# Denominator sums of a linear-attention block: four quarters of PE's columns in place of two halves

## The chip, the cores and the metric

The kernel runs on one core of one Trainium2 chip. The metric is the device time of one execution in microseconds (us). The kernel before the change takes 1488.77 us, the median of 3 runs (1488.16 to 1489.85). Engine names are those of the profile: PE is TensorE's matmul (PEld its weight load), DVE is VectorE, ACT is ScalarE, POOL is GpSimd, SP is SyncE, which issues most of the DMAs.

## The reference, cut to what matters

Everything is float32, S = 2048 tokens and D = 576 features.

```python
xn = layernorm(x)
q, k, v = split_heads(xn @ wqkv)              # H = 32 heads of 18
phi = lambda t: where(t > 0, t + 1, exp(t)) + 1e-6
pq, pk = phi(q), phi(k)
kv  = einsum("hsd,hse->hde", pk, v)
z   = einsum("hsd->hd", pk)
num = einsum("hqd,hde->hqe", pq, kv)
den = einsum("hqd,hd->hq", pq, z) + 1e-6
s   = merge_heads(num / den) @ wo
g   = silu((gelu(xn @ w_gate) * (xn @ w_up)) @ w_down)      # 4608 wide
out = x + s * g
```

The change touches den, one number for each head and token (32 x 2048), and the division by it.

## The kernel before, in words

**Stages.** Up to about 190 us the kernel norms x, multiplies it with the k and v weights and sums kv and z over all tokens in one PSUM accumulation (kv_a, kv_b). In between and up to 231 us it computes q for four blocks of TBN = 512 tokens, and phi of it. At about 197 to 210 us kv is masked to its heads and multiplied with wo (kv_wo, L525), which gives the operand kvh, kvl and kv4 (high and low words, see below), and z is spread on the heads' columns: zc, a matrix with one column for each head. From 231 to 303 us the kernel divides phi(q) by den and multiplies it with that operand: that is s, stored in DRAM. From 303 to 1104 us follow the gate and up projections (with Winograd-like sums of blocks, names al, be, ga, de), and from then to the end the down projection (bd) and the output.

**Precision.** The large products use the one-pass type fp32r on words: ACT copies an operand with rounding (the high word), DVE subtracts it from the original (the low word), and PE adds up the products of the words. Products on plain f32 operands, den's among them, are told by the trace as two matmul instructions, each with a weight load of its own, for every matmul that the kernel writes.

**The division.** Features of q lie on the 128 rows (partitions) in NHG = 5 groups, tokens along the columns. For each block of tokens `den` (L612) is called once, `scale` (L634) for each of the five groups, `halve` (L642) to split the scaled phi(q) into words.

- `den` multiplies zc (128 rows x 64 columns) with phi(q) of the group, 5 groups added up in PSUM. The 64 columns of zc hold the 32 heads twice (the write of zc at the end of kv_wo has r = 2). The two halves of a block's tokens, HB = 256 each, go to the two halves of PE's columns: rows 0 to 63 of the PSUM bank d get the first half of the tokens, rows 64 to 127 the second, each half with its 32 sums twice, one copy below the other.
- DVE adds EPS to the bank into r (128 x 256) and takes the reciprocal.
- For each half, ACT copies the 64 rows into rd (in the tile aux) at the half's own columns, rounding to fp32r, and DVE overwrites the lower 32 rows of them with the low word, r minus the high word. So rd (128 x 512) holds on 32 rows the high words and on the 32 rows beside them the low words of one half, and zeros at the other half's columns, which `make_sel` (L574) writes once with POOL.
- `scale` multiplies rd with sel, a matrix of zeros and ones that adds up all rows of a head and spreads them on the head's features, into a bank b, and DVE multiplies phi(q) with it.

**Order.** Every engine gets its instructions in the order in which the kernel writes them (the helpers act, vec, mm, pool and dma, L121 to L134, pin each to the program's order). Around the change that order is written out by hand: den(2) stands after the first of the five products q of block 3, and scale(2) after the third, fourth and fifth (q_hold, L458); den(3), den(0) and den(1) stand each after the first of the four products s of the block before (s_mm, L662, 28 matmuls on two banks), with the scales after the second and third. Between them stand the builds of operands for the gate stage (xf to xo, 'T1', 'T2'). make_sel is called behind the last q of block 2. The PSUM banks d, b, q and s come from one rotation of six.

The four calls of den share one tile rd, and every helper's instructions have one line in the profile (L128 for PE, L125 for DVE, L122 for ACT, L131 for POOL, L134 for DMAs), so they are told apart by tiles.

Of the kernel before, what the change touches and what calls it, by code (L numbers as in the profile page):

```python
# [8 lines left out]
F32 = mybir.dt.float32  # L9
# [3 lines left out]
ALU = mybir.AluOpType  # L13
# [3 lines left out]
P = 128  # L17
# [3 lines left out]
H = 32  # L21
# [4 lines left out]
TBN = S // TB  # L26
# [4 lines left out]
NHG = 5  # L31
WIDTHS = [GW, GW, GW, GW, D - 4 * GW]
W4 = WIDTHS[4]


Q4 = 64
# [54 lines left out]
def block_kernel(ctx, tc, x, xe, wq_d, wkv_d, wo, wgu_d, wd_d, out):  # L91
# [6 lines left out]
    def bank(name):  # L98
        return ps.tile([P, 512], F32, tag="one", bufs=6, name=name)
# [4 lines left out]
    def big(i, shape, dt, name):  # L104
        return sb.tile(shape, dt, tag=f"b{i}", bufs=1, name=name)
# [7 lines left out]
    def gl_tile(shape, name, dt=F32):  # L113
        return sb.tile(shape, dt, tag="gl", bufs=6, name=name)

    def tmp(shape, name):
        return sb.tile(shape, F32, tag="tmp", bufs=4, name=name)
# [3 lines left out]
    def act(*args, **kw):  # L121
        pin(nc.scalar.activation(*args, **kw))  # L122

    def vec(op, *args, **kw):
        pin(getattr(nc.vector, op)(*args, **kw))  # L125

    def mm(*args, **kw):
        pin(nc.tensor.matmul(*args, **kw))  # L128

    def pool(op, *args, **kw):  # L130
        pin(getattr(nc.gpsimd, op)(*args, **kw))  # L131

    def dma(out, in_, eng=None):
        tc.keep_in_program_order((eng or nc.sync).dma_start(out=out, in_=in_))  # L134

    def split(hi, lo, src):
        act(hi, src, AF.Copy)
        vec("tensor_sub", lo, src, hi.bitcast(F32))
# [1 line left out]
    ident = sb.tile([P, P], F32, name="ident")  # L140
    make_identity(nc, ident)
    eps_t = sb.tile([P, 32], F32, name="eps_t")
    eps_t, zx = eps_t[:, 0:1], eps_t[:, 2:4]
    small = sb.tile([P, 640], F32, name="small")
    nc.gpsimd.memset(eps_t, LN_EPS)

# [321 lines left out]
    at = {}  # L468

    def band(m, src, pattern, c):  # L470
        nc.gpsimd.affine_select(
            out=m, in_=src, compare_op=ALU.is_ge, fill=0.0, base=0,
            pattern=[[-s, n] for s, n in pattern], channel_multiplier=c,
        )
        nc.gpsimd.affine_select(
            out=m, in_=m, compare_op=ALU.is_ge, fill=0.0, base=DH - 1,
            pattern=[[s, n] for s, n in pattern], channel_multiplier=-c,
        )

    def make_masks():  # L480
        ones = tmp([P, NHG * H], "ones")
        nc.gpsimd.memset(ones, 1.0)

        at["mask"] = mask = small[:, 0:GW]
        m3, o3 = (i.rearrange("p (h j) -> p h j", h=HG) for i in (mask, ones[:, 0:GW]))
        nc.gpsimd.affine_select(
            out=m3, in_=o3, compare_op=ALU.is_ge, fill=0.0, base=-1,
            pattern=[[-DH, HG], [0, DH]], channel_multiplier=1,
        )
        nc.gpsimd.affine_select(  # L490
            out=m3, in_=m3, compare_op=ALU.is_ge, fill=0.0, base=DH,
            pattern=[[DH, HG], [0, DH]], channel_multiplier=-1,
        )
        nc.gpsimd.memset(mask[0:1, :], 1.0)
        at["maskh"] = small[:, P : P + NHG * H].rearrange("p (g h) -> p g h", g=NHG)
        band(at["maskh"], ones.rearrange("p (g h) -> p g h", g=NHG), [[-GW, NHG], [DH, H]], 1)
        at["zc"] = small[:, P + NHG * H : P + 3 * NHG * H].rearrange("p (g h) -> p g h", g=NHG)
        nc.gpsimd.memset(at["zc"][Q4:P], 0.0)

    def kv_done():  # L500
# [24 lines left out]
    def kv_wo(gi):  # L525

        if gi == 4:
            at["kvh"] = big(4, [P, 4, D], F32R, "kvh")
            at["kvl"] = big(5, [P, 4, D], F32R, "kvl")

            at["kv4"] = big(6, [P, 4, D], F32R, "kv4")
            pool("memset", at["kv4"][Q4:P, 1, :].bitcast(F32), 0.0)
        kvh, kvl, kv4 = at["kvh"], at["kvl"], at["kv4"]
        zc, mh = at["zc"], at["maskh"]
        wdt, k = (W4, W4 + 1) if gi == 4 else (GW, GW + 1)
        w = at["wo4"] if gi == 4 else at["wo"][:, gi]
        pw = []
        for c, cs in enumerate((slice(0, HALF), slice(HALF, D + 2))):
            pw.append(bank(f"kw_{gi}_{c}"))
            mm(  # L540
                pw[c][0:wdt, 0 : cs.stop - cs.start], at["kvm"][0:k, gi, 0:wdt], w[0:k, cs],
                start=True, stop=True,
            )
        r, x_ = slice(0, Q4 if gi == 4 else GW), slice(Q4, W4)
        z = pw[1][:, HALF : HALF + 1]

        def parts(hi, lo, rows):
            for c in range(2):
                cs = slice(c * HALF, (c + 1) * HALF)
                split(hi[:, cs], lo[:, cs], pw[c][rows, 0:HALF])  # L550

        if gi == 4:
            vec("tensor_copy", zx[x_], z[x_].to_broadcast([W4 - Q4, 2]))
            parts(kv4[x_, 2, :], kv4[x_, 3, :], x_)
            for c in range(2):
                act(kv4[Q4:P, 0, c * HALF : (c + 1) * HALF], pw[c][r, 0:HALF], AF.Copy)

        vec(
            "tensor_scalar", zc[r, gi, :].rearrange("p (r h) -> p r h", r=2),
            mh[r, gi, None, :].to_broadcast([r.stop, 2, H]), z[r], None, op0=ALU.mult,  # L560
        )
        if gi == 4:
            parts(kv4[r, 0, :], kv4[r, 1, :], r)
        else:
            parts(kvh[r, gi, :], kvl[r, gi, :], r)

    def move_rows():
        for gi in range(4):
            r, e = slice(Q4 + 2 * gi, Q4 + 2 * gi + 2), slice(GW, P)
            dma(out=at["zc"][e, gi, :].rearrange("p (r h) -> p r h", r=2)[:, :, H - 1], in_=zx[r])  # L570
            for t, i in ((at["kvh"], 2), (at["kvl"], 3)):
                dma(out=t[e, gi, :].bitcast(F32), in_=at["kv4"][r, i, :].bitcast(F32))

    def make_sel():  # L574

        n = NHG * P
        buf = big(15, [P, n + TBN], F32R, "aux")
        at["sel"] = sel = buf[:, 0:n].rearrange("p (g j) -> p g j", g=NHG)
        at["rd"] = rd = buf[:, n : n + TBN]
        one = sb.tile([H, NHG, P], BF16, tag="tmp", bufs=4, name="self")  # L580
        pool("memset", one, 1.0)
        four, last = one[:, 0:4, 0:GW], one[:, 4, :].rearrange("p (r j) -> p r j", r=2)
        for o, pattern, base in ((four, [[GW, 4], [1, GW]], 0), (last, [[0, 2], [1, Q4]], 4 * GW)):
            pool(
                "affine_select",
                out=o, in_=o, compare_op=ALU.is_ge, fill=0.0, base=base,
                pattern=pattern, channel_multiplier=-DH,
            )
            pool(
                "affine_select",  # L590
                out=o, in_=o, compare_op=ALU.is_ge, fill=0.0, base=DH - 1 - base,
                pattern=[[-s_, n_] for s_, n_ in pattern], channel_multiplier=DH,
            )
        pool(
                "affine_select",
            out=one[:, 0:4, GW:P], in_=one[:, 0:4, GW:P], compare_op=ALU.is_ge, fill=0.0,
            base=1 - H, pattern=[[0, 4], [0, P - GW]], channel_multiplier=1,
        )
        for i in range(4):
            r = slice(i * H, (i + 1) * H)  # L600
            if i % 2:
                act(sel[r], one, AF.Copy)
            else:
                pool("tensor_copy", sel[r], one)
        for i in range(2):
            pool(
                "memset", rd[2 * H * i : 2 * H * (i + 1), HB * (1 - i) : HB * (2 - i)].bitcast(F32), 0.0
            )

    HB = TBN // 2  # L610

    def den(tb):  # L612

        pd = bank(f"d_{tb}")
        for gi in range(NHG):
            for i in range(2):
                mm(
                    pd[2 * H * i : 2 * H * (i + 1), 0:HB], at["zc"][:, gi, :],
                    ph[tb][:, gi, i * HB : (i + 1) * HB],
                    start=(gi == 0), stop=(gi == NHG - 1),  # L620
                )
        r = gl_tile([P, HB], f"r_{tb}")
        rd = at["rd"]
        vec("tensor_scalar", r, pd[:, 0:HB], EPS, None, op0=ALU.add)
        vec("reciprocal", r, r)
        for i in range(2):
            c = slice(i * HB, (i + 1) * HB)
            rows, low = slice(2 * H * i, 2 * H * (i + 1)), slice(H * (2 * i + 1), 2 * H * (i + 1))
            act(rd[rows, c], r[rows], AF.Copy)
            vec("tensor_sub", rd[low, c], r[low], rd[low, c].bitcast(F32))  # L630

    pqs, s_d, words = {}, {}, {}

# [629 lines left out]
    center(3)  # L1263
    v_post(1, 2)
    make_masks()

    def x_next(n):
# [22 lines left out]
    for n in range(3, 2 * TT):  # L1290
# [3 lines left out]
        if n >= TT:  # L1294
            j, c = divmod(n - TT, 2)
# [102 lines left out]
    for q in range(NQ):  # L1398
        g = q // 2
# [61 lines left out]
```

## Time and profile before

| what | value |
|---|---|
| median of 3 runs | 1488.77 us |
| profiled execution, its own time | 1488.81 us |
| its span, first to last instruction | 1487.1 us |
| mean granted TensorE clock | 0.998 |
| tile d on PE | 80 matmuls of 128x256, 215.1 to 275.4 us |
| DVE reciprocal | 4 of 1753 ns |

How to read it: the span is what the profile sees; the profiled execution's own time has 1.7 us more around it. Busy shares are those of the span. A row of a timeline has the start, the length from the first start to the last end, the engine, line and operation, out<-in tiles, the shape, and a count; in brackets stands the engine's idle time before it, and what ended it. A row of a tile view has the count, the shortest, median and longest duration in ns, and the first and last start. Matmuls are pipelined: each is longer than the distance to the next, so the distance of starts tells what one costs. A row of the chain of waits has a start, a length and who held the chain; SPq is SP's DMA queue.

### The profile page before, as it was taken

The page shows a single profiled execution, that of the slowest core. Times are in us where ns is not written, and L with a number is a line of the kernel's source. Part 1 is how long each engine was busy: PE and PEld are TensorE (multiplying, and loading weights), DVE is VectorE, ACT ScalarE, POOL GpSimd, SP SyncE. Part 2 cuts the span into 40 slices and gives each one's busy share as a digit, 9 for nine tenths or more (in the row PEclk, how much of TensorE's full clock was granted, in tenths as well). Part 3 has the DMA queues.
Part 4 walks back from the last instruction along what each step waited for, and adds up shares of the span by engine and source line. Part 5 has one row for each costly group of instructions (what it writes and reads, how often), then busy time and mean ns, then how long its engine had stood idle before and what let it go on. Part 6 is the DMA issues. An engine that isn't in the chain of part 4 may idle for free.

```text
span 1487.1 us, 21863 instructions
## 1 busy us (share of the span) xinstructions
PE 1471.1 (99%) x8128; PEld 1310.2 (88%) x8128; DVE 1145.7 (77%) x1587; ACT 560.1 (38%) x923; POOL 581.0 (39%) x515
## 2 busy tenths in 40 slices
PE   8999999999999999999999999999999999999998
PEld 8989988988888888888888888888889999999998
DVE  7567466557787788787878787788787988989887
ACT  5434335433223322323322223322234546455454
POOL 4342241124656757555675655757641000000000
PEclk9999999999999999999999999999999999999999
DMA  4425003452231522433242232422379888767886
GB/s 163 176 117 213 6 2 136 167 207 86 92 128 54 181 85 93 149 106 110 82 163 101 98 128 67 167 86 98 129 274 314 262 258 261 240 188 239 272 291 214
DMA packets 115132, 230.62 MB, mean 155 GB/s; under 512 B 10882, under 2 KB 42882, under 8 KB 112978
## 3 DMA queue, kind: packets, MB, share of 16 engines
q1 hardware_dynamic: 112370, 217.17, 43.5%
q0 software_dynamic: 2656, 12.06, 2.2%
q8 instruction: 64, 1.05, 0.3%
q14 instruction: 42, 0.34, 0.1%
HBM read 146.57 MB, written 82.58 MB: 154 GB/s over the span
## 4 chain that ended last, share of the span: by engine, by line
PE 95%; DVE 2%; DMA 1%; issue 1%; ACT 0%; SPq 0%; POOL 0%; DVEq 0%; POOLq 0%; ACTq 0%
PE bd L128 24%; PE ga L746 15%; PE de L746 15%; PE al L746 15%; PE kv L128 8%; PE be L746 7%; PE q L128 4%; PE s L128 4%; PE kv_a L128 1%; PE xt L205 1%; PE d L128 1%; DMA raw<-in_wgu_dram 0%; DVE wb L125 0%; DMA raw_b<-hs 0%; PE kw L128 0%
## 5 line engine op out<-in xcount | busy, mean ns | idle before, releaser
L131 POOL TENSOR_TENSOR sm<-raw 128x384 f32<-128x384 f32 x72 | 76.7, 1065 | 154.6 <-DMA raw<-in_wgu_dram 129.0
L128 PE MATMUL kv<-wkv,xo_B 128*128 128x384 f32 x672 | 127.6, 346 | 0.3 <-ACT xo_B L122 0.3
L125 DVE TENSOR_TENSOR wa<-sm,wa 128x768 fp32r<-128x768 f32 x72 | 93.0, 1291 | 36.1 <-ACT wa L122 35.3
L128 PEld LDWEIGHTS kv<-wkv,xo_B 128*128 128x128 f32 x672 | 119.4, 193 | 1.2 <-ACT xo_B L122 0.8
L128 PE MATMUL bd<-w_head,hi 128*128 128x288 f32 x516 | 118.0, 294 | 0.0
L125 DVE TENSOR_TENSOR wb<-raw,wb 128x256 fp32r<-128x256 f32 (+1 forms) x108 | 108.0, 1000 | 7.3 <-ACT wb L122 5.8
L125 DVE TENSOR_TENSOR wa<-raw,wa 128x256 fp32r<-128x256 f32 x72 | 64.8, 900 | 50.7 <-ACT wa L122 47.5
L122 ACT ACTIVATE hi<-raw_h 128x1024 fp32r<-128x1024 f32 x59 | 62.4, 1060 | 96.8 <-PE bd L128 64.0
L128 PE MATMUL bd<-w_end,hi 128*128 128x288 f32 x448 | 89.9, 294 | 0.0
L122 ACT ACTIVATE spot_h<-spot_h 128x512 f32<-128x512 f32 x49 | 30.8, 633 | 151.7 <-DVE spot_h L125 151.7
L125 DVE TENSOR_TENSOR raw_h<-raw_h,hi 128x1024 fp32r<-128x1024 f32 x59 | 71.7, 1219 | 20.6 <-ACT hi L122 20.5
L128 PEld LDWEIGHTS bd<-w_head,hi 128*128 128x128 f32 x516 | 87.0, 188 | 0.1
L128 PE MATMUL bd<-w_end,raw_h 128*128 128x288 f32 x264 | 77.9, 295 | 0.0
L122 ACT ACTIVATE u<-al 128x512 f32<-128x512 f32 x72 | 41.0, 592 | 90.1 <-PE al L746 81.8
L122 ACT ACTIVATE wa<-sm 128x1152 fp32r<-128x1152 f32 x36 | 41.8, 1161 | 81.6 <-PE de L746 71.0
L128 PEld LDWEIGHTS bd<-w_end,hi 128*128 128x128 f32 x448 | 71.9, 188 | 0.0
L128 PE MATMUL bd<-beside,raw_h 128*128 128x288 f32 x240 | 70.8, 295 | 0.0
L128 PE MATMUL q<-xo_B,wq 128*128 128x512 f32 x240 | 64.1, 395 | 0.0
L746 PE MATMUL ga<-xo_B,wb 128*128 128x512 f32 x252 | 63.3, 390 | 0.4 <-DVE u L125 0.4
L131 POOL TENSOR_TENSOR spot_h<-spot_h,spot_h 128x512 f32<-128x512 f32 x45 | 62.1, 1387 | 2.9 <-DVE spot_h L125 2.4
L746 PE MATMUL al<-xo_B,wa 128*128 128x512 f32 x252 | 63.0, 389 | 0.0
L746 PE MATMUL ga<-xr_B,wb 128*128 128x512 f32 x252 | 63.0, 389 | 0.0
(259 smaller groups left out, 4076.1 us busy)
## 6 DMA issues: line engine op xcount, KB each, us to landing
raw_h<-hs SPq DMA_DIRECT2D x176, 256.0 KB
raw<-in_wgu_dram SPq DMA_DIRECT2D x36, 768.0 KB
hs<-spot_h SPq DMA_DIRECT2D x90, 256.0 KB
hs<-spot_g SPq DMA_DIRECT2D x80, 256.0 KB
b<-in_wd_dram SPq DMA_DIRECT2D x42, 432.0 KB
hs<-spot_m SPq DMA_DIRECT2D x38, 256.0 KB
raw_g<-hs SPq DMA_DIRECT2D x22, 256.0 KB
kept_T<-xo_T SPq DMA_DIRECT2D x4, 1280.0 KB
```

The source lines that it names most:

```text
L122: pin(nc.scalar.activation(*args, **kw))
L125: pin(getattr(nc.vector, op)(*args, **kw))
L128: pin(nc.tensor.matmul(*args, **kw))
L131: pin(getattr(nc.gpsimd, op)(*args, **kw))
L205: pin(nc.tensor.transpose(xts[n][j][:, k, :], xs[:, j, k * P : (k + 1) * P], ident))
L746: nc.tensor.matmul(o, w[0:rows, wi, :], xop[0:rows, xi, :], start=(start and n == 0), stop=(n == len(PASSES) - 1), skip_group_check=True,)
```

## The change

den now cuts the 512 tokens of a block into four quarters of 128, one for each quarter (32 columns) of PE, and zc holds each head once. The bank d has 32 sums on each of four groups of 32 rows, r is 128 x 128. For each quarter ACT copies its 32 rows to rd at the quarter's own columns, and DVE writes the low words to the 32 rows beside it (the neighbour's rows, `i ^ 1`) at the same columns. rd is cleared whole. zc and the column of z that is moved by DMA have half the width.

The written matmuls of one den go from 10 (64 columns of weights, 256 tokens) to 20 (32 columns, 128 tokens), ACT's copies from 2 to 4, DVE's subtractions from 2 to 4. All else keeps its place in the order of its engine.

```diff
-    eps_t, zx = eps_t[:, 0:1], eps_t[:, 2:4]
+    eps_t, zx = eps_t[:, 0:1], eps_t[:, 2:3]
...
-        at["zc"] = small[:, P + NHG * H : P + 3 * NHG * H].rearrange("p (g h) -> p g h", g=NHG)
+        at["zc"] = small[:, P + NHG * H : P + 2 * NHG * H].rearrange("p (g h) -> p g h", g=NHG)
...
-            vec("tensor_copy", zx[x_], z[x_].to_broadcast([W4 - Q4, 2]))
+            vec("tensor_copy", zx[x_], z[x_])
...
         vec(
-            "tensor_scalar", zc[r, gi, :].rearrange("p (r h) -> p r h", r=2),
-            mh[r, gi, None, :].to_broadcast([r.stop, 2, H]), z[r], None, op0=ALU.mult,
+            "tensor_scalar", zc[r, gi, :], mh[r, gi, :], z[r], None, op0=ALU.mult,
         )
...
-            dma(out=at["zc"][e, gi, :].rearrange("p (r h) -> p r h", r=2)[:, :, H - 1], in_=zx[r])
+            dma(out=at["zc"][e, gi, H - 1 : H], in_=zx[r])
...
-        for i in range(2):
-            pool(
-                "memset", rd[2 * H * i : 2 * H * (i + 1), HB * (1 - i) : HB * (2 - i)].bitcast(F32), 0.0
-            )
-
-    HB = TBN // 2
+        pool("memset", rd.bitcast(F32), 0.0)
+
+    HB = TBN // 4
...
         for gi in range(NHG):
-            for i in range(2):
+            for i in range(4):
                 mm(
-                    pd[2 * H * i : 2 * H * (i + 1), 0:HB], at["zc"][:, gi, :],
+                    pd[H * i : H * (i + 1), 0:HB], at["zc"][:, gi, :],
                     ph[tb][:, gi, i * HB : (i + 1) * HB],
                     start=(gi == 0), stop=(gi == NHG - 1),
                 )
...
         vec("tensor_scalar", r, pd[:, 0:HB], EPS, None, op0=ALU.add)
         vec("reciprocal", r, r)
-        for i in range(2):
+        for i in range(4):
             c = slice(i * HB, (i + 1) * HB)
-            rows, low = slice(2 * H * i, 2 * H * (i + 1)), slice(H * (2 * i + 1), 2 * H * (i + 1))
+            rows, low = (slice(H * k, H * (k + 1)) for k in (i, i ^ 1))
             act(rd[rows, c], r[rows], AF.Copy)
-            vec("tensor_sub", rd[low, c], r[low], rd[low, c].bitcast(F32))
+            vec("tensor_sub", rd[low, c], r[rows], rd[rows, c].bitcast(F32))
```

## The prediction

> **What bounds the kernel now.** I read the page first (busy times and the chain that ended last), then the kernel in stretches, then the two tiles that the change touches, and last the timeline of each engine around one of the four calls of den.
>
> ```profile
> span 1487.1 us, 21863 instructions
> PE 1471.1 (99%) x8128; PEld 1310.2 (88%) x8128; DVE 1145.7 (77%) x1587; ACT 560.1 (38%) x923; POOL 581.0 (39%) x515
> ...
> PE 95%; DVE 2%; DMA 1%; issue 1%; ACT 0%; SPq 0%; POOL 0%; DVEq 0%; POOLq 0%; ACTq 0%
> PE bd L128 24%; PE ga L746 15%; PE de L746 15%; PE al L746 15%; PE kv L128 8%; PE be L746 7%; PE q L128 4%; PE s L128 4%; PE kv_a L128 1%; PE xt L205 1%; PE d L128 1%; DMA raw<-in_wgu_dram 0%; DVE wb L125 0%; DMA raw_b<-hs 0%; PE kw L128 0%
> ```
>
> PE is busy all the time, and the chain is 95% PE. Tile d, which den writes, is on that chain with 1%. The table by stretches shows where PE has any time to spare.
>
> ```profile
> 200.00:303.00 103.00, 102.94 (x669) 91.18 (x668) 60.09 (x96) 46.56 (x91) 21.89 (x28) 1.00 0.32 116
> 303.00:500.00 197.00, 197.00 (x872) 163.20 (x871) 143.29 (x199) 60.16 (x99) 105.32 (x86) 1.00 0.34 121
> ...
> 1090.00:1130.00 40.00, 35.69 (x222) 32.57 (x221) 35.85 (x39) 16.09 (x22) 16.89 (x23) 1.00 0.89 307
> ```
>
> After the length, the columns are PE, PEld, DVE, ACT and POOL busy, the granted clock, the DMA share and GB/s. All four dens lie in 200 to 303 us, where PE is busy for 102.94 of 103.00 us at clock 1.00. So a PE instruction taken out there shortens the run, as long as nothing else is late in its place.
>
> **What one den costs PE.** The tile view of d:
>
> ```profile
> L128 PEld LDWEIGHTS d<-ph,small x80: 132/137/138, 215.1 to 275.2; 128*64 128x64 f32 x80
> L128 PE MATMUL d<-ph,small x80: 378/379/431, 215.1 to 275.4; 128*64 128x256 f32 x80
> ...
>   DVE r L125: 7.4, 3
> ```
>
> Two stretches at the start of the first den, of tile d alone (PE, PEld, DVE):
>
> ```profile
> 215.06:215.08 0.02, 0.01 (x2) 0.01 (x2) 0.00 (x0) 1.00 0.00 0
> 215.08:215.30 0.22, 0.22 (x2) 0.18 (x4) 0.00 (x0) 1.00 0.00 0
> ```
>
> The timeline of PE, start and length first:
>
> ```profile
> 215.07 2.38 PE L128 MATMUL d<-ph,small 128*64 128x256 f32 x20
> 217.38 1.42 PE L128 MATMUL q<-xo_B,wq 128*128 128x512 f32 x5
> ...
> 201.50 2.11 PE L128 MATMUL kw<-wo_t,kvm 127*126 127x288 f32 x8
> ...
> 33.22 1.05 PE L128 MATMUL kv_a<-pk,va 128*127 128x126 f32 x8
> 34.10 0.29 PE L128 MATMUL kv_b<-pk,va 128*73 128x72 f32 x2
> ```
>
> The kernel writes 10 matmuls per den, 40 in all; the trace has 80, so each f32 matmul is two passes. From its first matmul to the next tile's, a den takes 217.38 - 215.07 = 2.31 us. What does a pass cost by its columns? Eight passes of kw take 2.11 us; with about 0.41 for the last, that is 1.70/7 = 0.243 us for 288 columns, 0.84 ns a column. Eight of kv_a with 126 columns: (1.05 - 0.27)/7 = 0.111, 0.88 ns a column. A pass of d with 256 columns should take 0.216 us, and 20 of them 4.3 us. They take half of it: the two halves of PE's columns work side by side. The stretches show it directly: two passes begin within 0.02 us, and no third one begins in the next 0.22.
>
> So a den is 10 slots of 0.216 us (2.16) and 0.15 us for the first weights and the change of shape at its end.
>
> **The change on PE.** A den now issues 20 matmuls, 40 passes of 128 columns, on four quarters. If the four work side by side as the two do, it is 10 slots of 0.11 us (kv_a's pass) and the same 0.15: 1.25 us, **1.06 us less**, wherever nothing else is late. Weights cost nothing of their own: the columns loaded per den stay 20 x 64 = 40 x 32, and they were hidden under the passes. The bounds: if no two quarters overlap, 40 x 0.11 + 0.15 = 4.55 us, 2.24 more than now; the good end is the 1.06 less. I take the good end: the nearest row, d itself, shows full overlap of its two parts, down to 0.216 against 0.216.
>
> **The change on DVE and ACT.** The tile view of r:
>
> ```profile
> L122 ACT ACTIVATE aux<-r x8: 414/417/418, 222.5 to 278.6; 64x256 fp32r<-64x256 f32 x8
> L125 DVE TENSOR_TENSOR aux<-r,aux x8: 415/418/423, 223.0 to 279.0; 32x256 fp32r<-32x256 f32 x8
> L125 DVE TENSOR_SCALAR r<-d x4: 411/425/425, 220.3 to 275.8; 128x256 f32<-128x256 f32 x4
> L125 DVE RECIPROCAL r<-r x4: 1753/1753/1754, 220.7 to 276.3; 128x256 f32<-128x256 f32 x4
> ```
>
> ACT, DVE and PEld around the first den, from their timelines:
>
> ```profile
> 217.53 1.49 ACT L122 ACTIVATE aux<-self 32x640 fp32r<-32x640 bf16 x2 [4.09 <-POOL self L131]
> ...
> 219.67 0.63 ACT L122 ACTIVATE e_q<-e_q 128x512 f32<-128x512 f32 x1
> ...
> 219.67 0.69 DVE L125 TENSOR_SCALAR ph<-q 128x512 f32<-128x512 f32 x1 [6.31 <-ACT e_q L122]
> 220.28 0.41 DVE L125 TENSOR_SCALAR r<-d 128x256 f32<-128x256 f32 x1
> ...
> 222.96 0.87 DVE L125 TENSOR_TENSOR aux<-r,aux 32x256 fp32r<-32x256 f32 x2 [0.48 <-ACT aux L122]
> ...
> 223.94 0.30 PEld L128 LDWEIGHTS b<-aux 128*128 128x128 f32 x2 [0.34 <-issue]
> ```
>
> With half the columns, DVE's add falls from 0.425 to about 0.29 (1.04 ns a column between this row and 0.69 at 512). The reciprocal is linear at best, 0.88, or 0.96 if 0.16 of it is fixed as in the add; I take 0.92. ACT's two copies become four: (0.63 - 0.417)/256 = 0.84 ns a column, so 0.31 each, 1.34 with the gaps against 0.86. The last subtraction falls from 0.42 to 0.29. DVE's four subtractions run behind the copies, one each. Sum of the chain from add to last low word: 0.14 + 0.83 + 0.13 - 0.48 = **0.62 us shorter**.
>
> That matters in the first den alone. In the other three DVE begins its add when PE is done (the 7.4 us, 3 times); the matrix product that follows den covers the chain already, and the chain gets shorter. In the first den DVE is held by its in-order queue: before the add stands ph, which starts at 219.67 after ACT's e_q, which stands behind two copies of self that ACT got from POOL at 217.53. Nothing of this moves when PE finishes d earlier. So the add still starts at 220.28, the low words are ready at 223.83 - 0.62 = 223.21, and b's weights load 0.11 later, at 223.32 against 223.94. PE would be there at 222.9, and waits about 0.45 us: **this den is worth 0.62, not 1.06**.
>
> **What is hidden or too small.** The five products for zc shrink, DVE has time there; the four row moves are as many, with half the elements; POOL clears rd in one memset in place of two, the same element count, long before ACT's first copy, which now waits for it. The order of the instructions on each engine is otherwise unchanged.
>
> **A stall that goes.** In the second and third den, building the next operand stands behind ACT's copies, and so does the product of ph and b, and then ACT's emptying of an s bank.
>
> ```profile
> 241.23 1.49 ACT L122 ACTIVATE xo_T<-xf_B 128x1536 fp32r<-128x1536 f32 x1
> ...
> 246.56 0.69 ACT L122 ACTIVATE s<-s 128x288 f32<-128x288 f32 x2
> ...
> 246.71 0.69 PE L128 MATMUL s<-kvh,pq 128*128 128x288 f32 x2
> 247.24 0.42 PE L128 MATMUL s<-kvl,pq 128*128 128x288 f32 x2
> 247.50 0.69 PE L128 MATMUL s<-kvh,pq 128*128 128x288 f32 x4
> ...
> 265.59 0.71 PE L128 MATMUL s<-kvh,pq 128*128 128x288 f32 x2
> ```
>
> Two passes at 246.71 and at 265.59 take the 0.69 and 0.71 us of four; 0.26 and 0.28 us are lost to a bank that ACT empties late. With ACT and DVE 0.5 us earlier against PE, I count both as gone: 0.54, at worst 0.
>
> **The sum.** 3 x 1.06 + 0.62 + 0.54 = 4.3 us. The profiled execution took 1488.81 us (span 1487.1 and 1.7 around it), which is 0.04 above the median of 1488.77. 1488.8 - 4.3 = **1484.5 us**, 0.29% less. From 303 us on everything is released by PE and moves with it.
>
> **Rivals.** *Two at a time.* If passes start only in the program's order, a quarter's second pass, which follows its first, holds back the next quarter; then each slot holds the second pass of one quarter and the first of the next, 21 slots of 0.11 in place of 10 of 0.216: 2.46 us with the 0.15, 0.15 more than now in each of four dens, and 0.5 won by the shorter chain. Time 1488.9. Against it: in the same order of passes the first slot of d would hold one pass and not two, and the stretches show two. The Trainium skill, page TensorE: Matmul & The Clock Gate, section Part 3 (packing small matmuls), states this very rule, strict first-in first-out for matmuls with only weight loads pulled ahead; by that rule the sum would be near nothing, and the two rows of this case disagree with it. Chance 0.10.
>
> *Overlap in part, or the gain given back.* A den now feeds 80 instructions (weights and passes) in 1.1 us, 14 ns each. The densest feed in the rows is kv_b's: (0.29 - 0.23) us for two instructions, 31 ns each, though its weights explain that too. At 31 ns a den is 2.48 + 0.15, 0.32 us more than now, time 1489.6; at 20 ns 1.75, time 1486.0. The other place is later:
>
> ```profile
> PE bd L128 <- DVE raw_a L125: 3.1, 2, 1.7
> ...
> PE bd L128 <- DVE raw_b L125: 1.2, 1, 1.2
> ...
> 1104.09 6.37 PE bd L128 x48
> 1110.46 0.02 issue
> 1110.48 0.32 SPq L134
> ...
> 1111.92 5.15 DMA raw_b<-hs
> ```
>
> Those 4.3 us wait for loads; if their end were fixed by the transfer alone, the gain would vanish there. But the chain shows the load issued after PE's own 48 passes, so it moves along. Chance of this group 0.16, spread over 1485.3 to 1489.6.
>
> *One at a time, the slow side.* Quarters may share a path that halves do not: four different token ranges are read at once from the same rows of ph, and the trace shows two at most. With no overlap: 4 x 2.24 - 0.5 = 8.5 us more, 1497.3. It is slower by over 0.2% (3.0 us) once a pass costs PE more than (2.16 + 3.5/4)/40 = 0.076 us on average, that is when fewer than 1.5 passes run side by side. Against it: the two halves overlap in full. Chance 0.10. This is also the case in which the change does not do what it says.
>
> **How the numbers follow.** Four side by side: 0.64, 1483.4 to 1485.8 (reciprocal and bank stalls at their bounds, and the runs' own spread, 1488.16 to 1489.85). With the partial group it reaches 0.80: the range is 1483.4 to 1488.0, and the other two cases are left out. A measurement of this kernel can tell about 0.2%, 3 us, from no change. Faster by more: 0.64 and a quarter of the partial group, 0.68. Within: the rest of it and two at a time, 0.22. Slower: 0.10.
>
> **What would show it.** In the changed profile d has 160 passes of 128x128 on 128*32. From d's first pass to the next tile's: 1.25 us means four at once, 2.3 two, 4.5 one. Four passes in the first 0.05 us confirm the order. b's weights idle at the first den, waiting for low words at about 223.3; a reciprocal near 0.92; ACT's copies near 0.31; no lost 0.26 before the last s product of the second and third den. I am wrong if d's stretch does not shrink, or if PE's idle time at 1113 to 1124 us grows by what was won.

## The result, and the profile after

The changed kernel takes 1484.67 us (median of 19 runs, 1483.92 to 1488.51), the kernel before 1488.77 in the same session (19 runs, 1487.77 to 1489.85): 4.10 us less, a ratio of 0.9978 with a 95% interval of 0.9971 to 0.9985. The predicted 1484.5 us is 0.17 us off, the predicted gain of 4.3 us is 0.2 too large. The nearness of the whole time owes something to luck: the runs of the changed kernel spread over 4.6 us, and the same kernel measured once more, below, gains 3.45 us.

The head of the page after, with its busy times:

```profile
span 1482.9 us, 22034 instructions
...
PE 1465.4 (99%) x8208; PEld 1307.9 (88%) x8208; DVE 1140.5 (77%) x1595; ACT 562.1 (38%) x931; POOL 581.5 (39%) x514
```

The span is 4.2 us shorter, and PE is busy 5.7 us less (1471.1 before). PE has lost more work than the run has lost time, so there is new waiting somewhere. The table by stretches shows some of it in the stage of the change, in the same 200 to 303 us as before:

```profile
200.00:303.00 103.00, 102.31 (x768) 93.28 (x767) 59.81 (x107) 50.78 (x105) 21.80 (x27) 1.00 0.35 126
```

PE's busy time falls from 102.94 to 102.31 of 103.00 us: 0.7 us of idle time in place of 0.06. The two tiles of the change, in the tile views of d and r (the row set in from the others is DVE's wait for d: 4.2 us in three dens, 7.4 before):

```profile
L128 PEld LDWEIGHTS d<-ph,small x160: 106/110/110, 214.7 to 270.6; 128*32 128x32 f32 x160
L128 PE MATMUL d<-ph,small x160: 272/273/297, 214.7 to 270.7; 128*32 128x128 f32 x160
...
  DVE r L125: 4.2, 3
```

```profile
L122 ACT ACTIVATE aux<-r x16: 306/308/310, 221.2 to 273.4; 32x128 fp32r<-32x128 f32 x16
L125 DVE TENSOR_TENSOR aux<-r,aux x16: 278/284/990, 221.6 to 274.7; 32x128 fp32r<-32x128 f32 x16
L125 DVE TENSOR_SCALAR r<-d x4: 281/290/291, 219.9 to 271.0; 128x128 f32<-128x128 f32 x4
L125 DVE RECIPROCAL r<-r x4: 953/953/953, 220.2 to 271.3; 128x128 f32<-128x128 f32 x4
```

Every median is near its forecast, but one of the 16 subtractions takes 990 ns where the median is 284. The waits of PE:

```profile
PE bd L128 <- DVE raw_a L125: 3.1, 2, 1.7
...
PE bd L128 <- DVE raw_b L125: 1.2, 1, 1.2
PE b L128 <- DVE aux L125: 0.6, 2, 0.5
```

The loads before the down projection cost the same 3.1 and 1.2 us as before, so nothing is given back there. New is the last row: b waits for the low words twice, where the prediction had it once.

**Where the 4.1 us come from.** From the first pass of d to the first of the gate stage (tile al) is a stretch that starts and ends with a PE instruction. PE's timeline of the kernel before has its end at

```profile
303.15 1.77 PE L746 MATMUL al<-xo_B,wa 128*128 128x512 f32 x7
```

It was 303.15 - 215.07 = 88.08 us; now it is 298.67 - 214.65 = 84.02, **4.06 us less**. (Outside it the two profiled executions differ both ways: d begins 0.4 us earlier now, the time from al to the first bd is 0.3 shorter, that from bd to the end 0.6 longer.) Following every PE instruction of the stretch in both traces, and noting where the distance between the pair jumps, gives the steps:

| step in the stretch | predicted | measured |
|---|---|---|
| PE's own time for four dens | 4 x -1.06 | 4 x -1.08 |
| first den: b waits for the low words | +0.44 (1.06 - 0.62) | +0.52 |
| second and third den: the late s bank | -0.54 in all | -0.26 and -0.28 |
| last den: b waits for the low words | 0 | **+0.33** |
| smaller steps | 0 | -0.05 |
| sum | -4.3 | -4.06 |

PE's timeline at the first den, where the late bank was, and at al:

```profile
214.65 1.30 PE L128 MATMUL d<-ph,small 128*32 128x128 f32 x40
215.88 1.42 PE L128 MATMUL q<-xo_B,wq 128*128 128x512 f32 x5
...
223.00 0.70 PE L128 MATMUL b<-aux 128*128 128x512 f32 x2 [0.47 <-DVE aux L125]
...
244.65 0.42 PE L128 MATMUL s<-kvh,pq 128*128 128x288 f32 x2
...
298.67 1.77 PE L742 MATMUL al<-xo_B,wa 128*128 128x512 f32 x7
```

The first two starts are 1.23 us apart, against 2.31 before. Two s passes now start at 244.65 and take the usual 0.42 us; the same pair took 0.69 before.

The last den, on DVE, POOL and PE:

```profile
271.02 0.29 DVE L125 TENSOR_SCALAR r<-d 128x128 f32<-128x128 f32 x1 [1.04 <-PE d L128]
271.35 0.95 DVE L125 RECIPROCAL r<-r 128x128 f32<-128x128 f32 x1
272.73 2.24 DVE L125 TENSOR_TENSOR aux<-r,aux 32x128 fp32r<-32x128 f32 x4 [0.43 <-ACT aux L122]
```

```profile
270.12 1.00 POOL L131 TENSOR_TENSOR sm<-raw 128x384 f32<-128x384 f32 x1 [2.92 <-ACT s L122]
271.20 1.01 POOL L131 TENSOR_TENSOR sm<-sm,raw 128x384 f32<-128x384 f32 x1
272.16 1.01 POOL L131 TENSOR_TENSOR sm<-raw 128x384 f32<-128x384 f32 x1
273.14 1.06 POOL L131 TENSOR_TENSOR sm<-raw,sm 128x384 f32<-128x384 f32 x1
```

```profile
275.03 0.73 PE L128 MATMUL b<-aux 128*128 128x512 f32 x2 [0.17 <-DVE aux L125]
```

The four subtractions of this den take 2.24 us; in the first den four take 1.28. They begin at 272.73, in the middle of four sums on POOL: `mat_sums(0)`, the first sums for the gate stage (tile sm), which the kernel writes behind den(1). The first two subtractions take 0.585 and 0.990 us, and end 0.14 us after POOL's third and fourth sum (273.18 and 274.20). The reciprocal, which lies beside the second and third sum, has its usual 953 ns. In the kernel before the two did not meet, as the last of POOL's sums and DVE's subtractions there show:

```profile
276.88 1.01 POOL L131 TENSOR_TENSOR sm<-raw,sm 128x384 f32<-128x384 f32 x1
```

```profile
278.59 0.87 DVE L125 TENSOR_TENSOR aux<-r,aux 32x256 fp32r<-32x256 f32 x2 [0.54 <-ACT aux L122]
```

POOL ended at 277.89, DVE began 0.7 us later. Both now come earlier, but POOL's sums, released by an ACT copy of s, by 3.7 us, and the subtractions, behind the shorter den and reciprocal, by 5.9. The shorter chain ran into its neighbour. The Trainium skill, page SBUF — State Buffer, section SBUF: two separate sides, states that DVE and GpSimd share a pair of ports as an exclusive lock for a whole instruction, among other cases when a DVE operation with two SBUF inputs meets a GpSimd operation that reads SBUF; this trace agrees: the two-input subtractions take 0.30 and 0.71 us more than the usual 0.284 and end 0.14 us after a sum of POOL, while the one-input reciprocal is not held up.

### The profile page after: what moved, and what is told of

It is laid out like the page before. It is cut to its first block, busy times and chain, and to the rows that moved or that the text cites. A ratio compares the mean times of both kernels' runs of the same rounds, so it can differ in the third digit from the quotient of the medians.

```text
span 1482.9 us, 22034 instructions
## 1 busy us (share of the span) xinstructions
PE 1465.4 (99%) x8208; PEld 1307.9 (88%) x8208; DVE 1140.5 (77%) x1595; ACT 562.1 (38%) x931; POOL 581.5 (39%) x514
## 3 DMA queue, kind: packets, MB, share of 16 engines
q8 instruction: 65, 1.06, 0.3%
## 4 chain that ended last, share of the span: by engine, by line
PE 92%; DVE 3%; DMA 2%; POOL 1%; issue 1%; ACT 1%; SPq 0%; DVEq 0%; POOLq 0%; ACTq 0%
PE bd L128 23%; PE ga L742 15%; PE de L742 15%; PE al L742 14%; PE kv L128 8%; PE be L742 7%; PE q L128 4%; PE s L128 4%; PE kv_a L128 1%; PE xt L205 1%; DMA raw_h<-hs 0%; DMA hs<-spot_g 0%; DVE wa L125 0%; DMA raw_b<-hs 0%; POOL spot_h L131 0%
## 5 line engine op out<-in xcount | busy, mean ns | idle before, releaser
L742 PE MATMUL al<-xr_B,wa 128*128 128x512 f32 x252 | 63.0, 389 | 0.0
```

Source lines behind the costliest of these rows:

```text
L742: nc.tensor.matmul(o, w[0:rows, wi, :], xop[0:rows, xi, :], start=(start and n == 0), stop=(n == len(PASSES) - 1), skip_group_check=True,)
```

## The experiments

Ratios are to the kernel before on the same chip, with their 95% interval. "The stretch" is the one above, from the first pass of d to the first of al: 88.08 us before, 84.02 after. The diffs are to the changed kernel unless said otherwise.

**The changed kernel again.** 

> The changed kernel once more, unchanged. What is open is the spread: most of its runs lie at 1483.9 to 1484.8 us, some at 1485.9 to 1488.5. If that is a second way in which this kernel can run, some runs of this one lie near 1488 again and a profile of one has a stall of 3 to 4 us that the other profile has not. If it is chance of the chip that day, they lie within 1 us of 1484.6.

Measured: 1485.78 us (11 runs, 1483.77 to 1487.83) against 1489.23, ratio 0.9978 (0.9969 to 0.9986). Its profile is of one of the longer executions, span 1486.1 us, and so tells where the runs of this kernel differ. PE's timeline of that execution, at four landmarks (first pass of kv_b, of d, of al and of bd):

```profile
35.22 0.29 PE L128 MATMUL kv_b<-pk,va 128*73 128x72 f32 x2
...
216.25 1.30 PE L128 MATMUL d<-ph,small 128*32 128x128 f32 x40
...
300.27 1.77 PE L742 MATMUL al<-xo_B,wa 128*128 128x512 f32 x7
...
1100.79 0.42 PE L128 MATMUL bd<-w_head,hi 128*128 128x288 f32 x2
```

kv_b starts 1.53 us later than in the first profile of this kernel (33.69), and the stretch is 84.02 us, the same to 0.01. The rest of the 3.2 us is behind the gate stage: from the first bd to the end it takes 1486.1 - 1100.8 = 385.3 us against 383.8. Both places show a lower granted clock in the longer execution. The stretches 17 to 21 us, and the four us behind PE's wait for loads in the down projection, first in the first profile of the changed kernel, then in this one:

```profile
17.00:21.00 4.00, 4.00 (x18) 4.00 (x18) 3.77 (x10) 0.27 (x1) 0.00 (x0) 0.72 0.49 188
1118.60:1122.60 4.00, 3.92 (x29) 3.92 (x30) 4.00 (x6) 0.83 (x1) 0.74 (x2) 1.00 0.95 330
...
17.00:21.00 4.00, 4.00 (x13) 4.00 (x14) 3.78 (x10) 1.47 (x2) 0.00 (x0) 0.50 0.55 197
1120.30:1124.30 4.00, 3.96 (x18) 3.96 (x19) 4.00 (x5) 0.00 (x0) 0.78 (x2) 0.57 0.85 297
```

PE's waits there are the same (3.1 and 1.2 us), but behind them 14 passes start 0.24 us apart in place of 0.13, which is the 1.5 us at the end. At the start the lower clock goes with the other 1.5 us, which was not taken apart. So the longer execution shows no stall of 3 us; what it lost lies outside the stretch, and the stretch is the sharper measure for the rest of this section.

**The two parts of the change, each by itself.** With PE's four quarters, but a longer chain on DVE: the reciprocal is taken once more into columns that nobody reads.

```diff
-        r = gl_tile([P, HB], f"r_{tb}")
+        rr = gl_tile([P, 2 * HB], f"r_{tb}")
+        r = rr[:, 0:HB]
...
+        vec("reciprocal", rr[:, HB : 2 * HB], r)
         vec("reciprocal", r, r)
```

> The changed kernel with each reciprocal done twice (once into columns that nothing reads), so that the chain from d to the low words has about its old length again, while PE has its four quarters. If PE's quarters carry the gain: 3 x 1.08 us on PE stay, the first den loses its 0.5 to 1 us to the wait for the low words, and the waits of b and of the s banks come back with 0.2 to 0.5 us each; about 1486.5 us. If the shorter reciprocal carries it: back to 1488 or more.

Measured: 1488.88 us, ratio 0.9996 (0.9987 to 1.0005); stretch 86.99 us. The waits of PE in this kernel:

```profile
PE b L128 <- DVE aux L125: 2.1, 3, 1.5
```

The four dens still take 1.229 us each. But the chain is 0.98 us longer in the first three dens (0.28 in the last, where only one subtraction now meets POOL's sums), and that costs 2.97 us of the 4.06: b comes late in every den (by 1.50, 0.30, 0.36 and 0.62 us against the kernel before), and the late s banks are back. I had sized that too small, and had taken the chain for about its old length. It is longer than that. DVE's add and subtractions of the second den, first in the kernel before, then in this one:

```profile
238.10 0.42 DVE L125 TENSOR_SCALAR r<-d 128x256 f32<-128x256 f32 x1 [3.20 <-PE d L128]
240.80 0.87 DVE L125 TENSOR_TENSOR aux<-r,aux 32x256 fp32r<-32x256 f32 x2 [0.48 <-ACT aux L122]
...
236.96 0.29 DVE L125 TENSOR_SCALAR r<-d 128x128 f32<-128x128 f32 x1 [2.15 <-PE d L128]
239.60 1.28 DVE L125 TENSOR_TENSOR aux<-r,aux 32x128 fp32r<-32x128 f32 x4 [0.38 <-ACT aux L122]
```

From the add to the last low word it was 3.56 us and is 3.92; over the four dens the chain is 0.42, 0.36, 0.36 and 0.61 us longer than in the kernel before. The waits of b in the second to fourth den are about this surplus. So the 1.09 us that this kernel still gains is not what PE's quarters bring by themselves. An estimate from these figures: with the old length the first den would gain nothing and the other three 1.08 us each, 3.2 in all, before POOL's sums are met.

And the other way round: the kernel before (diff to that), with the reciprocal of the first 128 columns only; that of the other 128, half of the tokens, is left out.

```diff
-        vec("reciprocal", r, r)
+        vec("reciprocal", r[:, 0 : HB // 2], r[:, 0 : HB // 2])
```

> The kernel before, halves on PE, with the reciprocal of the first 128 columns of r alone (the reciprocal of half of the tokens is left out). If PE's quarters carry the gain: only the two late s banks (0.26 and 0.28 us) and 0.1 us at the first b go, 1488.2 us. If the shorter chain carries it: near 1485.

Measured: 1488.69 us, ratio 0.9997 (0.9988 to 1.0006); stretch 87.15 us, dens of 2.31 as before. The shorter reciprocal is worth 0.93 us by itself: 0.19 at the first den's b, 0.26 and 0.28 at the two s banks, and smaller steps. That shows that the stalls at the banks went with DVE's chain and not with PE's quarters. With the estimate of 3.2 for PE's quarters that makes 4.1 us, near the measured 4.06, but no run has the quarters with a chain of just the old length. What is shown is that PE's gain turns into waits of b as soon as the chain is a few tenths of a us longer than it was.

**The order of the passes on PE.** The prediction let four quarters work side by side, and named the strict order of passes as a rival. Two stretches of tile d at the first den of the changed kernel (PE, PEld, DVE):

```profile
214.64:214.68 0.04, 0.03 (x4) 0.03 (x4) 0.00 (x0) 1.00 0.00 0
214.68:214.78 0.10, 0.10 (x4) 0.10 (x8) 0.00 (x0) 1.00 0.00 0
```

Four passes start within 0.03 us (214.654 to 214.674) and none in the next 0.10. In the program each of the four quarters' first passes is followed by that quarter's second, so passes do start out of the program's order. How far? With the two loops changed over, all ten passes of one quarter stand in a row:

```diff
-        for gi in range(NHG):
-            for i in range(4):
+        for i in range(4):
+            for gi in range(NHG):
```

> The changed kernel with the two loops of den swapped: all five groups of the first quarter, then of the second, and so on. The same 40 passes per den; the second quarter's first pass now stands 20 instructions behind the first quarter's, the fourth's 60. If the quarters run apart from each other as far as PE looks ahead, and that is some 64 instructions: a den still takes 1.2 to 1.4 us, time within 0.7 us of the changed kernel. If PE looks only as far as one group of four (16 instructions): one quarter after the other, 40 x 0.09 + 0.2 = 3.8 us per den, some 8 to 10 us more than the changed kernel.

Measured: 1491.67 us, ratio 1.0018 (1.0009 to 1.0028); stretch 90.98 us, a den of 3.264 us. That lies between the two numbers expected. Three stretches of tile d in the first den:

```profile
214.87:215.54 0.67, 0.66 (x6) 0.67 (x7) 0.00 (x0) 1.00 0.00 0
215.55:216.23 0.68, 0.68 (x12) 0.68 (x11) 0.00 (x0) 1.00 0.00 0
216.24:216.92 0.68, 0.68 (x12) 0.68 (x11) 0.00 (x0) 1.00 0.08 24
```

Six passes alone; then in each of the next two stretches ten passes start, eight of them two by two and two alone (the counts of 12 take in two passes that began before). Each quarter's first pass starts (215.561, 216.246, 216.931) just after the quarter before it starts its seventh of ten, when three are still waiting. So three passes that can't start yet do not hold back another quarter, and a fourth does. In 0.109 us slots the den has 28.

My theory from that was that three waiting passes, of whatever quarters, may be overtaken. An order with two groups of each quarter, then two, then one, has four passes of a quarter in a row and would have 13 slots by it:

```diff
-        for gi in range(NHG):
+        for gs in ((0, 1), (2, 3), (4,)):
             for i in range(4):
+                for gi in gs:
```

> The changed kernel with den's loops in another order: groups 0 and 1 of the first quarter, then of the second, third, fourth, then groups 2 and 3, then group 4. Theory from the order quarter by quarter (28 slots, where the next quarter begins as soon as three passes of the one before are left): a pass may start past waiting passes, three of them at most. Counting with that gives 13 slots of 0.109 us and 0.24: 1.66 us per den. If two may be passed, 16 slots, 1.98 us; if four, 12 slots, 1.55; if the whole den, 10 slots, 1.33 or the 1.23 of now. The stretch is then 85.3 us with three.

Measured: 1485.12 us, ratio 0.9976 (0.9967 to 0.9985); stretch 84.04 us, a den of 1.266: 10 slots, as in the changed kernel, and not 13. That theory fell. What fits all three orders is a queue for each quarter: PE takes passes in the program's order into the queue of their quarter, which holds one running and three waiting passes, and takes no pass of any quarter while the next one finds its queue full. Counted by this rule the orders have 10, 28 and 10 slots (1.09, 3.05 and 1.09 us), which leaves 0.14, 0.21 and 0.18 us for the two ends of a den. It was tried on a fourth order, three groups of each quarter and then two, `for gs in ((0, 1, 2), (3, 4))`, where it gives 16 slots:

> den's loops with groups 0 to 2 of each quarter in turn, then groups 3 and 4. Theory A: PE feeds its instructions in order into a queue for each quarter, with room for one running and three waiting passes; when a quarter's queue is full the feed stops. It counts 28 slots for quarter by quarter and 10 for two groups, as measured, and 16 slots for this one: 1.98 us per den, stretch 86.5 us. Theory B: PE looks ahead over one list of waiting passes, far enough for two groups (9 waiting passes before the fourth quarter's first): then this order has 15 waiting and gives 14 slots or fewer, 1.75 us or less, stretch 85.6 us or less, and quarter by quarter should have given 19 slots and not 28.

Measured: 1487.05 us, ratio 0.9988 (0.9979 to 0.9997); a den of 1.955 us, which is 16 slots (1.74) and 0.21 for the ends. The rival named with it, one list of waiting passes for all quarters, gave 14 slots or fewer, 1.75 us, and falls. The stretches of tile d at the start of the first den:

```profile
214.68:214.90 0.22, 0.22 (x2) 0.22 (x3) 0.00 (x0) 1.00 0.00 0
214.93:215.10 0.17, 0.17 (x6) 0.17 (x5) 0.00 (x0) 1.00 0.00 0
```

Two passes of one quarter alone, and the second quarter starts with the first one's third pass (214.927 after 214.921): of six passes in a row one runs, three wait, and the other two are taken as the second and the third of that quarter start. The time of the stretch, 85.82 us, is under the expected 86.5. There I had added four times 0.73 us of longer den to 84.02; but where b waits for the low words anyway, in the first and the last den, a longer den costs nothing until that wait is used up, about 1.1 us in all (0.52 and 0.33 of new waits, and 0.19 and 0.08 that the kernel before lost there already).

**The first den's wait of b.** q_mm(3, 0) runs den(2) between its matmuls and its phi, and no longer behind both, so that DVE's add is not behind ph in its queue:

```diff
     q_hold(3, 8, [
-        [lambda: den(2)],
+        [],
...
-    ])
+    ], [lambda: den(2)])
```

> The changed kernel with the first den's matmuls, add, reciprocal and words written ahead of phi of the q product before them, so that DVE no longer stands behind ACT's copies of self when d is ready. The stretch from the first pass of d to the first pass of the gate stage is 84.02 us in both profiles of the changed kernel. If DVE's place in line is what holds back the first den: b's wait of 0.52 us and the 0.11 after it go, 83.4 us. If the length of the chain itself holds it: 84.0.

Measured: 1485.59 us, ratio 0.9973 (0.9964 to 0.9982); stretch 83.26 us, and no wait at the first den's b. So this wait came from den's place in the queue of DVE, as the prediction said (the edit moves ACT's copies ahead as well). It is worth 0.76 us: the 0.52 that the change added, and 0.19 that the kernel before lost at the same place (0.05 are not placed).

**The last den's wait of b.** The theory: POOL's sums hold up DVE's subtractions. To take them apart, mat_sums(0) moves in the program from behind den(1) to the end of that block, ahead of the load "T1":

```diff
-        (0, 0): [lambda: den(1), lambda: mat_sums(0)],
+        (0, 0): [lambda: den(1)],
...
-        (0, 3): [lambda: back("T1")],
+        (0, 3): [lambda: mat_sums(0), lambda: back("T1")],
```

> The changed kernel with POOL's four sums sm moved from behind the last den to two products of s later. If they slow DVE's subtractions of the last den (585 and 990 ns in place of 285): these take 285 ns each, b's wait of 0.33 us goes with the 0.11 behind it, and the stretch falls from 84.02 to 83.6 us. If the long subtractions have another cause they stay, and so does the stretch.

> Both of these edits. If the two waits are separate, the stretch is 83.0 us, and PE waits nowhere for a b of a den: the four dens then bring PE all of 4 x 1.08 us and the two late s banks. In time 1.0 us under the changed kernel, less than the spread of its runs.

Measured: 1484.69 us, ratio 0.9972 (0.9962 to 0.9981), stretch 84.01, for the move alone; 1484.57 us, ratio 0.9968 (0.9956 to 0.9981), stretch 83.25, for both edits. The second differs from den ahead of phi by nothing: the move had no effect. POOL's timeline of the first of the two shows why:

```profile
270.36 1.00 POOL L131 TENSOR_TENSOR sm<-raw 128x384 f32<-128x384 f32 x1 [2.91 <-ACT s L122]
...
273.37 1.06 POOL L131 TENSOR_TENSOR sm<-raw,sm 128x384 f32<-128x384 f32 x1
```

The sums ran when they ran before (its first den starts 0.25 us later): POOL has nothing else between the two places, so a later place in its program is no later time. The experiment told nothing on the theory. To delay the sums, something that waits must stand ahead of them. Behind the load "T1", which POOL issues and which waits for PE's last s, they do come later (with den ahead of phi as well):

```diff
-        (0, 3): [lambda: back("T1")],
+        (0, 3): [lambda: back("T1"), lambda: mat_sums(0)],
```

> The first den ahead of phi, as in the earlier run (stretch 83.26 us), and POOL's four sums written behind POOL's own load of T1, which it issues some 14 us after the last den; the earlier move left POOL idle between and so they ran at the same time as ever. If the sums are what lengthens DVE's subtractions of the last den: 16 subtractions of 285 ns, no wait of b in any den, stretch 82.8 us. If not: 990 ns stay, 83.3 us.

Measured: 1484.23 us, ratio 0.9965 (0.9952 to 0.9979); stretch 82.82 us, where 82.8 was expected. POOL's timeline and the tile view of r in this kernel:

```profile
283.26 0.53 POOL L134 DMA_DIRECT2D xr_T<-kept_T  x1 [16.45 <-PE s L128]
283.80 1.02 POOL L131 TENSOR_TENSOR sm<-raw 128x384 f32<-128x384 f32 x1
```

```profile
L125 DVE TENSOR_TENSOR aux<-r,aux x16: 280/283/289, 219.9 to 273.3; 32x128 fp32r<-32x128 f32 x16
```

With the sums 13 us later no subtraction is over 289 ns, and no wait of b is left. So the collision is what cost the 0.33 us. This version is 1.2 us better than the changed kernel in the stretch; in the whole time the intervals of the two overlap (0.9952 to 0.9979 and 0.9971 to 0.9985), so that there it isn't settled.

## Why the prediction was right, and where it was not

- **PE: right.** 10 slots of 0.109 us, 1.23 us a den where 1.25 was forecast. The step that carried it, reading from the kernel before that two passes of different halves start within 0.02 us, held for four quarters. The page of the Trainium skill that the prediction named (TensorE: Matmul & The Clock Gate, Part 3) has matmuls start and end in the order of the program; the four starts in 0.03 us and the orders above differ from it in the starts of passes of different quarters (of the ends no run here tells, since they are modelled). What the prediction lacked is that this depends on the written order: the same 40 passes in another order take 1.95 or 3.26 us, the last of which is slower than before.
- **"Two at a time": excluded** by the same starts. **"Overlap in part": excluded**, 80 instructions are fed in 1.1 us, 14 ns each. **"One at a time": excluded.** **"The gain given back at 1113 to 1124 us": excluded**, the waits there are unchanged.
- **First den: right.** Forecast 0.62 for the den, measured 1.08 - 0.52 = 0.56. The reciprocal was mis-sized in small, 0.953 us in place of 0.92: the other bound held, with a part that doesn't shrink with the columns.
- **The s banks: right**, 0.53 us where 0.54 was counted, and the kernel before with half the reciprocal shows that it was the chain that freed them.
- **The last den: wrong.** The step "In the other three DVE begins its add when PE is done; the matrix product that follows den covers the chain already, and the chain gets shorter" failed there: the chain got longer at its end, since its subtractions moved onto POOL's sums, and it came 0.33 us late. The prediction weighs ACT, DVE and PE beside the chain, at one den, and says nothing of POOL's sums beside the last. Counted, the sum would have been 4.0 us.
- **What the prediction did not say** is how thin the cover of the chain is. In the kernel before, b's first pass of the second, third and fourth den starts 0.14, 0.07 and 0.08 us behind the last low word; in the changed kernel 0.74 and 0.68 us in the second and third. So the prediction's 3 x 1.06 us on PE hold only with a chain no longer than the old one, and a chain 0.98 us longer than the new one takes back 2.97 us.
- **A slip without effect:** "the same element count" for POOL's clearing of rd. The two memsets of 64x256 became one of 128x512, twice the elements; it takes 0.53 us in place of 0.65 for the two and ends 2.0 us ahead of ACT's first copy.

What stays open: the smaller steps (0.05 us), and why the runs of the changed kernel spread over 4.6 us (1483.92 to 1488.51) where those of the kernel before spread over 2.1. In the one longer execution profiled the clock was lower at the start and behind the loads; whether that makes the other long ones, and what decides it, is not known. The drop behind the loads is in three of the ten profiles with four quarters and in neither of the two with halves, too few to tell the change apart from chance.

## What to carry to other kernels

Where a gain on the busiest engine has a chain on other engines behind it, follow the chain to its end at each place it occurs, with what runs beside it then on every engine: shortening it changes its neighbours. Small matmuls on several parts of PE's columns should be written in turn, part by part, with no more than a few passes of one part in a row (here four in a row cost 0.04 us a den, six 0.73, ten 2.04). And an instruction moved later in an idle engine's program does not run later; only what it waits for delays it.

## What the runs showed of the hardware

- Passes on different quarters of PE's columns start out of the program's order as far as a queue of one running and three waiting passes for each quarter lets them. The rule was made from three orders (10, 28 and 10 slots; 1.229, 3.264 and 1.266 us a den) and gave the fourth (16; 1.955). That it is a queue inside PE is an inference from the starts.
- A pass of 128 f32 columns on a quarter costs a slot of 0.109 us, and four share it: 0.027 us each.
- A DVE subtraction of 32x128 took 0.585 and 0.990 us beside POOL's sums of 128x384, and 0.284 without them; the reciprocal beside them took 0.953 as elsewhere.
- DVE's reciprocal takes 1753 ns for 256 f32 columns and 953 for 128: as a straight line through the two, 6.25 ns a column and some 0.15 us fixed.
- Behind 4.3 us of waits in the down projection, the granted clock was 0.57 over four us in one execution of the changed kernel and 1.00 in another, with PE's passes 0.24 and 0.13 us apart.
